# Attention with mixed heads and a gated feed-forward: keys loaded in rows of 768 bytes and transposed in seven pieces per pair, the last value rows loaded once and copied

## The chip, the cores and the metric

The kernel runs on one core of a Trainium2 chip. The metric is device time in microseconds (us) of one execution. Five engines of the core matter: TensorE (PE; its weight loads are shown apart as PEld), VectorE (DVE), ScalarE (ACT), GpSimd (POOL) and SyncE (SP), which here issues nearly all DMAs from one queue, in program order. A DMA that has to wait for a semaphore holds up every DMA behind it in that queue.

## The reference

```
scores = scale * q @ k^T                          # 4 batches, 12 heads, 448 positions, head size 64
scores = einsum('bhij,hg->bgij', scores, w_pre)   # heads are mixed before the softmax
attn   = softmax(scores)
attn   = einsum('bhij,hg->bgij', attn, w_post)    # and after it
x      = attn @ v                                 # as 1792 tokens x 768
out    = (silu(x @ w_gate) * (x @ w_val)) @ w_out # 768 -> 1536 -> 768
```

All inputs and the output are float32.

## The kernel before

Attention comes first (to about 411 us), batch by batch; the feed-forward part fills the rest. In attention the scores q k^T of all heads (`qk`, L275) are copied to SBUF (`stg`) and stored to DRAM (`s_all`, L294), so that they can be read back with heads and positions together on the partitions. `gather` (L305) reads the scores of 20 positions, a unit `u`, into a tile `rs`; a batch has 23 units. `pre` (L324) mixes the heads of the unit on TensorE, `top` and `expo` (L335, L341) make the softmax, `post` (L368) mixes the heads again and turns the result, and `av` (L410) multiplies by the values.

The keys of two heads, a pair, are loaded by `load_k` (L205; tile `kn`): 384 positions of the 448, three to a partition, and the last 64 of all heads in a load of their own (L192, and L202, tile `kl`). `kprep` (L228) turns a pair into the layout that `qk` wants, with transposes on TensorE into the PSUM tile `ktr`: three of 128x128 and one for the last 64 positions. `kcopy` takes the result to SBUF. There are 6 pairs in a batch and 24 in all.

The load of a pair before writes each partition in the order position, head, 64 numbers; a run of DRAM that stays together on both sides has 64 numbers, 256 bytes, so a pair has 128 x 6 = 768 such packets. The values (`load_v`, L170 and L176; tile `vn`) come in four loads of 384 positions in packets of 768 bytes, and two loads of the last 64 positions, one to partitions 0 to 63 and one to 64 to 127, in packets of 256 bytes (64 x 12 = 768 packets each), because `av` needs these rows on both halves.

The order of the program is a list of times written by hand: each step stands under a key, `at(key, fn)`, and the steps are sorted by it. A unit has two key units. Batch `b` starts at key `n0 = 45 b`; the keys of batch `b + 1` are loaded and turned during units 10 to 15 of batch `b`, and the values of batch `b` are loaded at keys `n0 + 16.2` to `n0 + 24.2`, so both loads meet in the same stretch of the SP queue with the gathers and the score stores. For batch 0 the keys of all pairs, the queries and the values are loaded in a prologue (negative keys) that ends with the first gathers.

Of the kernel before, what the change touches and what calls it, by code (L numbers as in the profile page):

```python
# [11 lines left out]
F32 = mybir.dt.float32  # L12
# [12 lines left out]
def talking_heads_moe_kernel(ctx, tc, q, k, v, w_pre, w_post, w_gate, w_val, w_out, out):  # L25
    nc = tc.nc
# [3 lines left out]
    P = 128  # L30
# [118 lines left out]
                wpost[half].rearrange("p g s -> p s g"), wq, n, op=ALU.mult  # L149
            )  # L150

    qn, kn, vn, kk, qt, stg, rs, pts, sts, et, rw, ats, trs, qtrs, qks = ({} for _ in range(15))


    def keys(c):
        return min(P, S - c * P)
# [7 lines left out]
    def load_v(b, c):  # L164
        full = S - PART
        if b not in vn:
            vn[b] = vp.tile([P, H, NC, D], F32, tag="vn", name=f"vn_{b}")
        if c < NC:
            hs = slice(c * (H // NC), (c + 1) * (H // NC))
            nc.sync.dma_start(  # L170
                out=vn[b][:, hs, :NC - 1].rearrange("p h c d -> p h (c d)"),
                in_=v[b, hs, :full].rearrange("h (p c) d -> p h (c d)", c=NC - 1),
            )
        else:
            r = c - NC
            nc.sync.dma_start(  # L176
                out=vn[b][r * HB:(r + 1) * HB, :, NC - 1], in_=v[b, :, full:].rearrange("h p d -> p h d")
            )

    def load_q(b, c, eng=nc.sync):  # L180
        m = scored(c)
# [3 lines left out]
    def load_k(b, p, part=None, eng=nc.sync):  # L185
        full = S - PART
        n = (NC - 1) * 2 * D
        if b == 0:
            if "all" not in kn:
                kn["all"] = stp.tile([P, NPAIR * NC * 2 * D], F32, tag="stg", name="kn_0")  # L190
            if part == 1:
                eng.dma_start(  # L192
                    out=kn["all"][:PART, NPAIR * n:].rearrange("p (h d) -> p h d", d=D),
                    in_=k[b, :, full:].rearrange("h p d -> p h d"),
                )
                return
            t = kn["all"][:, p * n:(p + 1) * n]
            last = kn["all"][:PART, NPAIR * n + p * 2 * D:NPAIR * n + (p + 1) * 2 * D]
        else:
            if p == 0:  # L200
                kn["last"] = nat.tile([PART, H, D], F32, tag="kl", name=f"kl_{b}")
                nc.sync.dma_start(out=kn["last"], in_=k[b, :, full:].rearrange("h p d -> p h d"))  # L202
            t = nat.tile([P, n], F32, tag="kn", name=f"kn_{b}_{p}", bufs=3)
            last = kn["last"][:, 2 * p:2 * p + 2].rearrange("p h d -> p (h d)")
        eng.dma_start(  # L205
            out=t.rearrange("p (c j d) -> p (c j) d", j=2, d=D),
            in_=k[b, 2 * p:2 * p + 2, :full].rearrange("j (p c) d -> p c j d", c=NC - 1),
        )
        kn[b, p] = [t[:, c * 2 * D:(c + 1) * 2 * D] for c in range(NC - 1)] + [last]

    def first_act():
        t = smp.tile([P, 1], F32, tag="st", name="first_act", bufs=4)
# [7 lines left out]
    def kprep(b, p):  # L220
        kt = kn.pop((b, p))
        if b == 0:
            tr = ps.tile([P, S], F32, tag="pre" if p in (2, 3) else "post", name=f"ktr_{b}_{p}")
        else:
            tr = ps.tile([P, S], F32, tag="tr", bufs=2, name=f"ktr_{b}_{p}")
        for c in range(NC):
            m = keys(c)
            nc.tensor.transpose(tr[:, c * P:c * P + m], kt[c], ident[:m, :m])  # L228
        trs[b, p] = tr

    def kcopy(b, p):
# [156 lines left out]
    def av(b, c0, m, p):  # L388
        n = -(-cols(c0, m) // TS)
        w = SEG // (3 - m)  # L390
        pt = [ps.tile([P, S], F32, tag="tr", name=f"av_{b}_{c0}_{p}_{r}")[:, :SEG] for r in range(2)]
        first = (b * NC + c0) % NSEG
        wrapped = first + m > NSEG
        ring = attnT.rearrange("p (s u) z i -> p s u z i", s=NSEG)
        u0 = first * SU
        for c in range(NC):
            for x in range(3 - m):
                for r in range(2):
                    k = (n + 1 - r) // 2
                    part = slice(r * HB, (r + 1) * HB) if c == NC - 1 else slice(P)  # L400
                    for j in range(2):
                        h = 2 * (p + x) + j
                        js = slice(j * D, (j + 1) * D)
                        if wrapped:
                            o = pt[r][js].rearrange("p (s u i) -> p s u i", s=2, i=TS)
                            a = ring[part, 0:NSEG:NSEG - 1, :, place(r, c) + h]
                        else:
                            o = pt[r][js, x * SEG // 2:x * SEG // 2 + k * TS].rearrange("p (u i) -> p u i", i=TS)
                            a = attnT[part, u0:u0 + k, place(r, c) + h]
                        nc.tensor.matmul(o, vn[b][part, h, c], a, start=(c == 0 and x == 0), stop=(c == NC - 1 and x == 2 - m))  # L410
        avs[b, c0, p] = pt, c0, m, wrapped

    def spread(av, *to):
# [96 lines left out]
    for b in range(B):  # L510
# [2 lines left out]
        def slot(u):  # L513
            return (n0 if u >= 0 else n0 - NTB) + 2 * (u if u >= 0 else u + NUB)

        for i, c in enumerate((NC, NC + 1, *range(NC))):
            at(n0 + 16.2 + 1.6 * i if b else (-34.3, -34.29, -30.35, -30.34, -29.35, -29.34)[i], later(load_v, b, c))
        if b == 0:
            at(-61.0, later(load_q, b, 0, nc.scalar))
            at(-60.9, first_act)  # L520
# [603 lines left out]
```

## Time and profile before

| | |
|---|---|
| time, median of 3 runs | 906.1 us (905.49 to 907.57) |
| the profiled execution's own time | 903.57 us |
| its span, first to last instruction | 901.9 us |
| mean granted TensorE clock | 0.979 of 2.4 GHz |
| TensorE busy | 858.8 us, 95% of the span |
| DMA, mean over the span | 242 GB/s, 187537 packets, 58360 of them under 512 bytes |
| wait of TensorE for gathers / for keys | 13.6 us / 4.0 us |

The profile counts an engine as busy from the start to the modelled end of each instruction, so a TensorE that is busy all the time can still be at half its clock: the granted clock stands in a column of its own. The DMA share is the mean over the 16 DMA engines and can pass 1 where packets of two queues overlap.

### The profile page before, as it was taken

Reading aid. Unit: us, or ns where it says so; the run is one execution under the profiler, and the core shown is the slowest. Engines: PE = TensorE matmul, PEld = TensorE weight load, DVE = VectorE, ACT = ScalarE, POOL = GpSimd, SP = SyncE. Lnnn points to the kernel's source line nnn. Section 1 sums busy time; section 2 is a strip of 40 time slices with the busy share of each in tenths; the row PEclk is TensorE's granted clock in tenths of the full one; section 3 lists DMA queues with packets and bytes.
Section 4 is the critical chain, followed back from the end, with each engine's and each line's share of the span. In section 5 each row is a group of like instructions: output and inputs, shape, how many; then the busy total and the mean of one; then the engine's idle time right before and its main releaser. Section 6 shows DMA issues by size and latency. Waiting matters only on the chain.

```text
span 901.9 us, 26545 instructions
## 1 busy us (share of the span) xinstructions
PE 858.8 (95%) x10886; PEld 706.9 (78%) x10886; DVE 647.6 (72%) x1204; ACT 457.8 (51%) x1042; POOL 177.0 (20%) x257
## 2 busy tenths in 40 slices
PE   8579999899989998989999999999999998999998
PEld 5355676566656665768999999999999998999998
DVE  3466576567656756575999999678899978766853
ACT  3375677567656767654333333354554464353321
POOL 2111111111211111113544543111001121002020
PEclk9699999899979999999999999999999999999999
DMA  9899988998898779544778776446655578988696
GB/s 214 289 304 283 272 295 245 318 301 280 281 320 256 242 253 291 186 133 152 254 231 265 242 259 225 145 157 212 220 178 178 187 275 285 347 268 195 171 306 156
DMA packets 187537, 218.03 MB, mean 242 GB/s; under 512 B 58360, under 2 KB 155160, under 8 KB 187416
## 3 DMA queue, kind: packets, MB, share of 16 engines
q1 hardware_dynamic: 181448, 207.97, 72.0%
q0 software_dynamic: 2080, 5.51, 3.5%
q10 hardware_dynamic: 3888, 2.86, 1.2%
q8 instruction: 86, 1.41, 0.6%
q14 instruction: 35, 0.29, 0.1%
HBM read 136.77 MB, written 79.54 MB: 240 GB/s over the span
## 4 chain that ended last, share of the span: by engine, by line
PE 81%; DMA 6%; DVE 6%; ACT 3%; issue 2%; SPq 1%; POOL 0%; ACTq 0%; POOLq 0%; DVEq 0%
PE pre L324 8%; PE av L410 8%; PE post L368 7%; PE p L758 6%; PE p L755 6%; PE p L756 6%; PE q L899 5%; PE q L897 5%; PE q L898 5%; PE qk L275 5%; DMA rs<-s_all 4%; PE upv L811 3%; PE upv L810 3%; PE upv L814 3%; PE upg L814 3%; PE upg L810 3%
## 5 line engine op out<-in xcount | busy, mean ns | idle before, releaser
L341 ACT ACTIVATE e<-pre,st 128x448 f32<-128x448 f32 x180 | 112.6, 630 | 91.8 <-DVE st L335 91.6
L660 POOL TENSOR_SCALAR mag<-mag 128x768 f32<-128x768 f32 x33 | 101.1, 3065 | 259.8 <-ACT mag L658 237.3
L335 DVE TENSOR_REDUCE st<-pre 128x1 f32<-128x448 f32 x180 | 104.5, 619 | 62.6 <-PE pre L324 58.4
L324 PE MATMUL pre<-rs,w_pre_blocks 64*64 64x448 f32 (+1 forms) x720 | 110.1, 579 | 18.0 <-DMA rs<-s_all 13.6
L368 PEld LDWEIGHTS post<-rw,e 60*64 60x64 f32 x5040 | 99.4, 138 | 33.4 <-issue 25.6
L352 POOL TENSOR_SCALAR rw<-w_post_gs,st 128x60 f32<-128x60 f32 x180 | 55.1, 320 | 325.3 <-DVE st L349 234.7
L368 PE MATMUL post<-rw,e 60*64 60x60 f32 x5040 | 106.7, 224 | 7.0 <-issue 3.9
L383 ACT ACTIVATE attnT<-post 128x420 f32<-128x420 f32 (+1 forms) x192 | 91.1, 541 | 23.8 <-PE post L368 23.1
L897 PE MATMUL q<-ohi,ah 128*128 128x384 f32 x276 | 93.6, 339 | 1.6 <-ACT ah L890 1.6
L899 PE MATMUL q<-ohi,al 128*128 128x384 f32 x276 | 93.8, 340 | 1.0 <-DVE al L882 1.0
L275 PE MATMUL qk<-kk,qt 64*64 64x448 f32 x672 | 93.4, 544 | 0.3 <-DVE w_post_gs L148 0.3
L898 PE MATMUL q<-olo,ah 128*128 128x384 f32 x276 | 93.5, 339 | 0.0
L410 PE MATMUL av<-attnT,vn 128*64 128x120 f32 (+9 forms) x1728 | 88.8, 262 | 3.0 <-DVE st L348 1.4
L410 PEld LDWEIGHTS av<-attnT,vn 128*64 128x64 f32 (+1 forms) x1728 | 70.4, 136 | 15.3 <-issue 5.6
L284 DVE COPY stg<-qk 128x448 f32<-128x448 f32 x120 | 71.1, 618 | 9.0 <-PE qk L275 4.2
L890 ACT ACTIVATE ah<-ar 128x768 fp32r<-128x768 f32 x46 | 38.6, 844 | 55.5 <-PE q L898 31.5
L275 PEld LDWEIGHTS qk<-kk,qt 64*64 64x64 f32 x672 | 32.2, 135 | 34.9 <-issue 24.1
L882 DVE TENSOR_TENSOR al<-ar,ah 128x768 fp32r<-128x768 f32 x46 | 43.9, 953 | 16.1 <-ACT ah L890 16.1
L324 PEld LDWEIGHTS pre<-rs,w_pre_blocks 64*64 64x64 f32 (+1 forms) x720 | 29.0, 138 | 33.2 <-issue 16.4
L899 PEld LDWEIGHTS q<-ohi,al 128*128 128x128 f32 x276 | 52.4, 190 | 2.0 <-DVE al L882 1.9
L897 PEld LDWEIGHTS q<-ohi,ah 128*128 128x128 f32 x276 | 52.3, 189 | 1.9 <-ACT ah L890 1.9
L810 PE MATMUL upv<-x,whi 128*128 128x448 f32 x144 | 52.8, 367 | 0.0
(142 smaller groups left out, 1688.5 us busy)
## 6 DMA issues: line engine op xcount, KB each, us to landing
rs<-s_all SPq DMA_DIRECT2D x88, 448.0 KB, 5.6
s_all<-stg SPq DMA_DIRECT2D x60, 448.0 KB, 4.8
w_d<-w SPq DMA_DIRECT2D x36, 384.0 KB, 4.3
raw<-in_moe_w_gate_dram SPq DMA_DIRECT2D x12, 768.0 KB, 5.5
raw<-in_moe_w_val_dram SPq DMA_DIRECT2D x12, 768.0 KB, 6.2
raw<-in_moe_w_out_dram SPq DMA_DIRECT2D x12, 768.0 KB, 6.4
w<-w_d SPq DMA_DIRECT2D x24, 384.0 KB, 5.5
s_all<-stg SPq DMA_DIRECT2D x39, 224.0 KB, 5.0
```

The lines of the kernel that those rows point to most:

```text
L275: nc.tensor.matmul(pt[x][i * HB:(i + 1) * HB], qt[b, c][hs, p, r:r + HB], kk[b, p][hs], start=True, stop=True)
L324: nc.tensor.matmul(pt[r][x * HB:(x + 1) * HB], wpre[i], xs[i, x], start=True, stop=True)
L335: nc.vector.tensor_reduce(sts[b, u][:, 0, r:r + 1], pts[b, t], axis=AX.X, op=ALU.max, negate=True)
L341: nc.scalar.activation(e, pts.pop((b, t)), AF.Exp, bias=st[:, 0, r:r + 1], scale=1.0, accum_out=st[:, 1, r:r + 1])
L368: nc.tensor.matmul(ats[b, u][y][o * HB:(o + 1) * HB, to, :m], et[b, t][i, c * P + x * HB:c * P + (x + 1) * HB], rw[b, t][i, :, :m], start= ...
L383: nc.scalar.activation(attnT[:part, i, n0:n1, y * HS:y * HS + m], pt[:part, n0:n1, :m], AF.Copy)
L410: nc.tensor.matmul(o, vn[b][part, h, c], a, start=(c == 0 and x == 0), stop=(c == NC - 1 and x == 2 - m))
L660: eng.tensor_scalar(mag, mag, f32_of(0x38000000), f32_of(0x47EFFFFF), op0=ALU.max, op1=ALU.min)
L810: nc.tensor.matmul(pt, hi[:, c], xh[:, c, ts], start=(c == 0), stop=False)
L897: nc.tensor.matmul(pt, ahi, bhi, start=f == 0, stop=False)
L898: nc.tensor.matmul(pt, ahi, blo, start=False, stop=False)
L899: nc.tensor.matmul(pt, alo, bhi, start=False, stop=f == NFH - 1)
```

## The change

Three edits. `load_k` writes each partition in the order head, position, so that the three positions of a partition, 768 bytes, are one packet: 256 packets for a pair in place of 768. The two heads' rows of one position no longer stand side by side, so `kprep` makes each of the three 128-position blocks with two transposes: one of 128 columns, whose upper half is head 1's row and whose lower half is a neighbouring row that isn't wanted there, and one of 64 columns that writes head 0's row over the lower half. Together with the last 64 positions that is seven transposes for a pair in place of four. The last positions of the values get a tile of their own, `vl`; one load fills its lower half, and `copy_v` copies this half to the upper one, from SBUF to SBUF, at key 1.55 in batch 0 and `n0 + 26.0` in the others.

```diff
@@ load_v
-            vn[b] = vp.tile([P, H, NC, D], F32, tag="vn", name=f"vn_{b}")
+            vn[b] = vp.tile([P, H, NC - 1, D], F32, tag="vn", name=f"vn_{b}")
+            vl[b] = vp.tile([P, H, D], F32, tag="vl", name=f"vl_{b}")
...
-            r = c - NC
-            nc.sync.dma_start(
-                out=vn[b][r * HB:(r + 1) * HB, :, NC - 1], in_=v[b, :, full:].rearrange("h p d -> p h d")
-            )
+            nc.sync.dma_start(out=vl[b][:HB], in_=v[b, :, full:].rearrange("h p d -> p h d"))
+
+    def copy_v(b):
+        nc.sync.dma_start(out=vl[b][HB:], in_=vl[b][:HB])
@@ load_k
         eng.dma_start(
-            out=t.rearrange("p (c j d) -> p (c j) d", j=2, d=D),
-            in_=k[b, 2 * p:2 * p + 2, :full].rearrange("j (p c) d -> p c j d", c=NC - 1),
+            out=t.rearrange("p (j z) -> p j z", j=2),
+            in_=k[b, 2 * p:2 * p + 2, :full].rearrange("j (p c) d -> p j (c d)", c=NC - 1),
         )
@@ kprep
-        for c in range(NC):
-            m = keys(c)
-            nc.tensor.transpose(tr[:, c * P:c * P + m], kt[c], ident[:m, :m])
+        t, last = kt
+        for c in range(NC - 1):
+            to = slice(c * P, (c + 1) * P)
+            nc.tensor.transpose(tr[:, to], t[:, (NC - 2 + c) * D:(NC + c) * D], ident)
+            nc.tensor.transpose(tr[:D, to], t[:, c * D:(c + 1) * D], ident)
+        nc.tensor.transpose(tr[:, (NC - 1) * P:], last, ident[:PART, :PART])
@@ the keys of the steps
-        for i, c in enumerate((NC, NC + 1, *range(NC))):
-            at(n0 + 16.2 + 1.6 * i if b else (-34.3, -34.29, -30.35, -30.34, -29.35, -29.34)[i], later(load_v, b, c))
+        for i, c in enumerate((NC, *range(NC))):
+            at(n0 + 16.2 + 1.6 * (i and i + 1) if b else (-34.3, -30.35, -30.34, -29.35, -29.34)[i], later(load_v, b, c))
+        at(n0 + 26.0 if b else 1.55, later(copy_v, b))
```

On TensorE, in the prologue, the first pair of keys stands like this before, from the queries' transposes to the second pair (`ktr` is the PSUM tile that is written, `kn` the keys):

```order
L245 MATMUL qtr_0_0_189<-ident,qn_0_118 128x64 x3
L228 MATMUL ktr_0_194<-ident,kn_120 128x128 x3
L228 MATMUL ktr_0_194<-ident,kn_120 128x64
L228 MATMUL ktr_1_201<-ident,kn_120 128x128 x3
L228 MATMUL ktr_1_201<-ident,kn_120 128x64
```

and with the change like this:

```order
L249 MATMUL qtr_0_0_189<-ident,qn_0_118 128x64 x3
L230 MATMUL ktr_0_194<-ident,kn_120 128x128
L231 MATMUL ktr_0_194<-ident,kn_120 64x128
L230 MATMUL ktr_0_194<-ident,kn_120 128x128
L231 MATMUL ktr_0_194<-ident,kn_120 64x128
L230 MATMUL ktr_0_194<-ident,kn_120 128x128
L231 MATMUL ktr_0_194<-ident,kn_120 64x128
L232 MATMUL ktr_0_194<-ident,kn_120 128x64
```

Every pair has three more transposes, whose output is 64 partitions by 128, and full and half ones alternate.

On the SP queue, in the prologue, the loads of values stand between the score stores; before:

```order
L294 DMA s_all<-stg_0_0_226 64x896
L183 DMA qn_2_231<-in_q_dram 128x12x64
L176 DMA vn_233<-in_v_dram 64x12x64 x2
L294 DMA s_all<-stg_0_1_263 64x896
L170 DMA vn_233<-in_v_dram 128x3x192 x2
L294 DMA s_all<-stg_0_2_276 64x896
L170 DMA vn_233<-in_v_dram 128x3x192 x2
L305 DMA rs_0_289<-s_all 128x2x448
```

and with the change:

```order
L298 DMA s_all<-stg_0_0_235 64x896
L184 DMA qn_2_240<-in_q_dram 128x12x64
L176 DMA vl_243<-in_v_dram 64x12x64
L298 DMA s_all<-stg_0_1_281 64x896
L171 DMA vn_242<-in_v_dram 128x3x192 x2
L298 DMA s_all<-stg_0_2_294 64x896
L171 DMA vn_242<-in_v_dram 128x3x192 x2
L309 DMA rs_0_307<-s_all 128x2x448
```

One load of the last value rows is gone ahead of the second score store; the rest keeps its order.

On the same queue in batch 1, where the keys of batch 2 and the values of batch 1 are loaded, from the gather of unit 11 to that of unit 13; before:

```order
L305 DMA rs_11_2636<-s_all 128x2x448
L176 DMA vn_2638<-in_v_dram 64x12x64
L205 DMA kn_1_2661<-in_k_dram 128x6x64
L294 DMA s_all<-stg_3_2_2652 128x896
L176 DMA vn_2638<-in_v_dram 64x12x64
L305 DMA rs_12_2709<-s_all 128x2x448
L205 DMA kn_2_2729<-in_k_dram 128x6x64
L170 DMA vn_2638<-in_v_dram 128x3x192
L294 DMA s_all<-stg_3_3_2723 128x896
L305 DMA rs_13_2775<-s_all 128x2x448
```

and with the change:

```order
L309 DMA rs_11_2673<-s_all 128x2x448
L176 DMA vl_2676<-in_v_dram 64x12x64
L206 DMA kn_1_2699<-in_k_dram 128x2x192
L298 DMA s_all<-stg_3_2_2690 128x896
L309 DMA rs_12_2746<-s_all 128x2x448
L206 DMA kn_2_2766<-in_k_dram 128x2x192
L171 DMA vn_2675<-in_v_dram 128x3x192
L298 DMA s_all<-stg_3_3_2760 128x896
L309 DMA rs_13_2812<-s_all 128x2x448
```

The second load of last value rows is gone from its place right ahead of the gather of unit 12; the copy stands further down, between the gathers of units 16 and 17.

## Rows read from the trace of the kernel before

**Rows 1.** The page: DMA share in 40 slices, in tenths.

```profile
DMA  9899988998898779544778776446655578988696
```

**Rows 2.** Stretches: us; busy PE, PEld, DVE, ACT, POOL; granted clock, DMA share, GB/s.

```profile
22.00:44.00 22.00, 12.64 (x176) 6.31 (x175) 9.67 (x22) 7.97 (x22) 1.80 (x6) 0.69 0.89 296
60.00:75.00 15.00, 10.48 (x236) 6.63 (x232) 8.57 (x22) 7.67 (x21) 2.12 (x8) 1.00 1.13 336
145.00:175.00 30.00, 27.48 (x589) 17.05 (x589) 18.13 (x47) 19.87 (x59) 4.78 (x16) 0.89 1.03 309
240.00:270.00 30.00, 26.45 (x553) 16.66 (x549) 18.87 (x52) 18.19 (x52) 5.29 (x17) 0.84 1.04 313
340.00:360.00 20.00, 16.81 (x439) 10.62 (x432) 13.39 (x35) 15.17 (x40) 3.58 (x12) 0.99 0.95 303
411.00:740.00 329.00, 328.76 (x1695) 301.86 (x1692) 282.50 (x387) 142.62 (x215) 92.10 (x30) 1.00 0.66 212
```

**Rows 3.** Waits of TensorE in attention: total us, times, longest.

```profile
PE pre L324 <- DMA rs<-s_all: 13.6, 6, 7.9
PE ktr L228 <- DMA kn<-in_k_dram: 4.0, 3, 3.1
```

**Rows 4.** Timeline of TensorE in batches 1 and 2; idle time before in brackets.

```profile
163.65 0.98 PE L324 MATMUL pre<-rs,w_pre_blocks 64*64 64x448 f32 x8 [0.41 <-DMA rs<-s_all]
165.87 0.52 PE L228 MATMUL ktr<-ident,kn 128*128 128x128 f32 x3 [1.24 <-DVE st L335]
168.63 1.77 PE L324 MATMUL pre<-rs,w_pre_blocks 64*64 64x448 f32 x8 [0.88 <-DMA rs<-s_all]
259.83 1.01 PE L324 MATMUL pre<-rs,w_pre_blocks 64*64 64x448 f32 x8 [2.93 <-DMA rs<-s_all]
264.12 1.77 PE L324 MATMUL pre<-rs,w_pre_blocks 64*64 64x448 f32 x8
```

**Rows 5.** Timeline of SP in the two crowded stretches of batches 1 and 2.

```profile
156.36 1.01 SPq L176 DMA_DIRECT2D vn<-in_v_dram  x1
157.42 1.49 SPq L305 DMA_DIRECT2D rs<-s_all  x1
161.08 0.44 SPq L305 DMA_DIRECT2D rs<-s_all  x1
252.47 0.60 SPq L176 DMA_DIRECT2D vn<-in_v_dram  x1
```

**Rows 6.** Transposes: durations at L228 (ns, min/median/max); timeline in the prologue.

```profile
L228 PE MATMUL ktr<-ident,kn x78: 272/273/473, 6.6 to 276.6; 128*128 128x128 f32 x72, 64*128 64x64 f32 x6
...
11.22 0.51 PEld L228 LDWEIGHTS ktr<-ident,kn 64*128 64x128 f32 x4 [0.17 <-issue]
11.90 0.51 PEld L228 LDWEIGHTS ktr<-ident,kn 64*128 64x128 f32 x4 [0.17 <-issue]
14.48 0.87 PE L245 MATMUL qtr<-ident,qn 128*128 128x128 f32 x6
```

**Rows 7.** DMA queue 1 in 10:12, 16:18 and 20:22: packets, MB, share.

```profile
q1 hardware_dynamic: 1381, 0.35, 107.3%
...
q1 hardware_dynamic: 1503, 0.38, 96.5%
...
q1 hardware_dynamic: 693, 0.55, 86.1%
```

**Rows 8.** Timeline of DVE and SP in the prologue.

```profile
12.85 3.56 SPq L176 DMA_DIRECT2D vn<-in_v_dram  x2
...
13.92 1.38 DVE L284 COPY stg<-qk 128x448 f32<-128x448 f32 x2 [0.40 <-PE qk L275]
...
16.52 1.03 SPq L294 DMA_DIRECT2D s_all<-stg  x1
...
19.09 0.56 SPq L294 DMA_DIRECT2D s_all<-stg  x1
...
25.09 1.64 SPq L305 DMA_DIRECT2D rs<-s_all  x3
```

More of the change, by code (lines that the diff above doesn't have):

```diff
@@ L150, in mixing_blocks @@
             )
-    qn, kn, vn, kk, qt, stg, rs, pts, sts, et, rw, ats, trs, qtrs, qks = ({} for _ in range(15))
+    qn, kn, vn, vl, kk, qt, stg, rs, pts, sts, et, rw, ats, trs, qtrs, qks = ({} for _ in range(16))
     def keys(c):
@@ L170, in load_v @@
             nc.sync.dma_start(
-                out=vn[b][:, hs, :NC - 1].rearrange("p h c d -> p h (c d)"),
+                out=vn[b][:, hs].rearrange("p h c d -> p h (c d)"),
                 in_=v[b, hs, :full].rearrange("h (p c) d -> p h (c d)", c=NC - 1),
@@ L205, in load_k @@
         eng.dma_start(
-            out=t.rearrange("p (c j d) -> p (c j) d", j=2, d=D),
-            in_=k[b, 2 * p:2 * p + 2, :full].rearrange("j (p c) d -> p c j d", c=NC - 1),
+            out=t.rearrange("p (j z) -> p j z", j=2),
+            in_=k[b, 2 * p:2 * p + 2, :full].rearrange("j (p c) d -> p j (c d)", c=NC - 1),
         )
-        kn[b, p] = [t[:, c * 2 * D:(c + 1) * 2 * D] for c in range(NC - 1)] + [last]
+        kn[b, p] = t, last
     def first_act():
@@ L409, in av @@
                             a = attnT[part, u0:u0 + k, place(r, c) + h]
-                        nc.tensor.matmul(o, vn[b][part, h, c], a, start=(c == 0 and x == 0), stop=(c == NC - 1 and x == 2 - m))
+                        nc.tensor.matmul(o, vn[b][part, h, c] if c < NC - 1 else vl[b][part, h], a, start=(c == 0 and x == 0), stop=(c == NC - 1 and x == 2 - m))
         avs[b, c0, p] = pt, c0, m, wrapped
```

## The prediction, made before the changed kernel ran

> **What bounds the kernel now.** I read the page's line of DMA shares first, then a table by stretch, the waits of TensorE, and the timelines of TensorE and SP at the places that the first three point to. The feed-forward part can be set aside: from 411 to 740 us TensorE is busy 328.76 of 329 us at full clock [rows 2], and the change touches nothing there. In attention the DMA engines are busy nearly throughout [rows 1], and two things cost TensorE time. One is plain waiting: 13.6 us for gathers and 4.0 us for keys [rows 3]. The other is the granted clock: it is 0.69 in 22 to 44 us, 0.89 in 145 to 175 and 0.84 in 240 to 270 [rows 2]. The chip grants 2.4 or 1.2 GHz, so a mean of 0.89 over 30 us is 30 x 0.11 / 0.5 = 6.6 us at half clock, and 0.84 is 9.6 us. Rows 4 show what goes before: in batch 1 TensorE idles 0.41, 1.24 and 0.88 us, and the same eight matmuls of `pre` that took 0.98 us take 1.77 us behind it; in batch 2 it idles 2.93 us, and `pre` takes 1.77 us from 264.12 on [rows 4]. So a stall there is paid twice, as idle time and as half clock behind it.
>
> Both places are the stretches where the keys of the next batch and the values of this one are loaded: DMA share 1.03 and 1.04 [rows 2], and SP takes 1.01 us to issue one load of last value rows right ahead of the gather of unit 12, which itself takes 1.49 us [rows 5]. Batch 0 has its crowded stretch at 60 to 75 us: share 1.13, TensorE busy 10.48 of 15 us [rows 2], 3.1 us of it waiting for the first keys [rows 3]. In batch 3, 340 to 360 us, values are loaded but no keys: busy 16.81 of 20 us [rows 2].
>
> **Transposes.** 24 pairs get 3 more each, 72. Six transposes of 128x128 in a row take 0.87 us [rows 6]; five steps and a last one that runs 0.27 us (the median there) make (0.87 - 0.27) / 5 = 0.12 us from start to start; I take 0.11, since the first step of a row waits for its weights. A pair takes 11.90 - 11.22 = 0.68 us before [rows 6]: four at 0.11 are 0.44, and the rest, 0.24, is two changes of shape (full to 64-row and back), 0.12 us each. Whether a 64-column piece changes the shape of the array too, no row shows. If it doesn't, a pair costs 3 x 0.11 = 0.33 us more; if every alternation costs one, there are five changes more, 0.60, and a pair costs 0.93 us more. I take 0.33, nearest to the transposes that keep all 128 rows: 72 x 0.11 = 7.9 us over the kernel, 2.0 us for the keys of each batch. The upper end is 22 us.
>
> The Trainium skill, page "TensorEngine Tiling (Array Packing)", Key Properties and Restrictions, says that a change of tiling mode drains the engine, and that column tiling cannot be combined with the transpose mode for float32. The drain agrees with the 0.12 us of [rows 6]; by the second rule the 64-column piece runs on the whole array, without a change of shape, at the lower end, 7.9 us.
>
> **Key loads.** A packet of 256 bytes costs: 1381 packets in 107.3% of 16 engines for 2 us is 24.9 ns each at the end of the loads of keys and queries, and 1503 in 96.5% is 20.5 ns a little later; 693 packets of 790 bytes in the mean, in 86.1%, is 39.8 ns [rows 7]. So a pair takes 768 x 20.5 / 16 = 0.98 us of all DMA engines before and 256 x 39.8 / 16 = 0.64 after: 0.35 us less (0.56 by the dearer row), 2.1 us in a batch.
>
> The Trainium skill, page "DMA: Bandwidth & Descriptors", section "Why small descriptors are slow (HBM only)", puts a packet at one cycle for 32 bytes and about 3 more: 3 x 11 = 33 cycles before against 27 after. By that rule a load shrinks by 18%, 0.18 us as an estimate, half of what the rows give, and the time would end nearer to no change. The 24.9 ns against 39.8 [rows 7] speak for the larger figure.
>
> **Last value rows.** The second load is 768 packets of 256 bytes as well: 0.98 us of DMA less in each batch, and on SP one issue less (0.60 to 1.01 us in [rows 5]; two took 3.56 us in the prologue [rows 8]). The copy adds 192 KB in 64 packets: 0.55 MB took 0.861 x 2 us [rows 7], so 0.6 us, and one issue, 0.44 us like a gather's [rows 5]. In batches 1 to 3 it stands behind the crowded stretch, between the gathers of units 16 and 17, and `av` needs it 3.3 key units later, some 7 us (411 us are 180 key units); in batch 0 it stands at key 1.55 and `av` starts at 29.3. The gather of unit 17 goes out 0.4 us later for it, and its `pre` is due some six key units behind. I take no wait of TensorE for either. If it landed late, `av` would wait perhaps 1 to 2 us a batch.
>
> **Place by place**, with the sum.
>
> Prologue. The first gather goes out at 25.09 us, when the third score store, issued at 19.09, has landed [rows 8]. SP was the late one: its second store went out at 16.52, though the data were ready at about 14.6 (the first of the two copies that start at 13.92) [rows 8]. Without one load, SP is free near 14.6; but the six pairs' transposes, 18 x 0.11 = 2.0 us, delay the data, less the two waits for keys that the shorter loads end (4.0 - 3.1 = 0.9 us [rows 3]): 1.1 us, so data at 15.7, store 0.8 us earlier. The copy gives back 0.4 us on SP. Net -0.5 us (from +1 to -1.5, and more if the half-clock stretch shortens as well).
>
> Batch 0, 60 to 85 us: +2.0 us of transposes, the 3.1 us wait for the first keys shorter by about 1.0 (0.35 for the load itself, the rest its issue behind fewer packets). Net +1.0.
>
> Batch 1: ahead of the gather of unit 13 (issued at 161.08, its `pre` at 168.63 [rows 4, 5]) lie three key loads and the dropped value load: 3 x 0.35 + 0.98 = 2.0 us of DMA, and SP a little earlier. I take 2.2 of the idle time of 0.41 + 1.24 + 0.88 = 2.5 us [rows 4]. Transposes +2.0. Net -0.2, before the clock.
>
> Batch 2: two key loads and the value load lie ahead of the gather that TensorE waits 2.93 us for [rows 4]: 2 x 0.35 + 0.98 = 1.7. Transposes +2.0. Net +0.3, before the clock.
>
> Batch 3: no keys; the value load alone, -0.9.
>
> Clock. In batch 1 the 6.6 us at half clock are full of work: at full clock 3.3 us less. In batch 2 those from 264.12 to 270 us are, 5.9 us: 2.9 us less. I take one of the two dips as gone: -3.1.
>
> Sum: -0.5 + 1.0 - 0.2 + 0.3 - 0.9 - 3.1 = -3.4 us. The profiled execution took 903.57 us, 2.5 below the median of the runs, and I let the difference carry over: 903.57 - 3.4 = 900.2, and in the median 906.1 - 3.4 = 902.7 us.
>
> **Rivals.**
>
> Both dips go, and the half-clock stretch of the prologue, 22 x 0.31 / 0.5 = 13.6 us [rows 2], shortens by half a dip: -3.4 - 3.1 - 1.7 = -8.2, 897.9 us. For it speaks that TensorE's stalls in batch 1 are already short; against it, that the DMA stays the bound of these stretches (share 1.03 and 1.04 [rows 2]), so TensorE at full clock would run into the next gather.
>
> The stalls shrink, but the clock dips as before: -3.4 + 3.1 = -0.3, 905.8 us. If a part of the 20.5 ns is other queues' traffic and not the packet's size, and a load saves only half of 0.35 us, it ends here too: 6 x 0.17 = 1.0 us of relief less in each of three batches, a part of it on the path, up to 908.
>
> Slower: the transposes lie on the path in full. This is one mechanism, TensorE as the bound: if the gathers' landing is set by when their scores were stored and not by how full the DMA queues are, the relief of the queues buys nothing in batches 0 to 2 and the 7.9 us stay, less 1.4 for prologue and batch 3 (0.5 + 0.9): 912.6 us. It decides as soon as less than 2.0 us of idle time and half clock go from a crowded stretch. For it: between stretches TensorE has hardly any idle time, so any work that is not covered by a stall counts. Against: the transposes stand in just the stretches in which TensorE idles.
>
> Slower still: every alternation of full and half transposes costs a change of shape: 24 x 0.60 = 14.4 us on top of the forecast, 917.1 us. Nothing in the rows excludes it.
>
> The change not doing what it says is no case: packets and transposes are fixed by the program.
>
> **How the numbers follow.** Chances: forecast 0.38 (its own range 900 to 904.3), both dips gone 0.17 (894 to 900), dips stay 0.22 (904 to 908), transposes on the path 0.15 (908 to 914), changes of shape 0.08 (914 and more). The range of 8 in 10 leaves out the lower third of the second case and the upper part of the last two: 896 to 911 us. Within 0.2%, 904.3 to 907.9 us, is about what a measurement of this kernel cannot tell from no change. Faster: 0.38 + 0.17 + 0.05 of the third = 0.60. Same: the rest of the third, 0.17. Slower: 0.15 + 0.08 = 0.23.
>
> **What the profile after would show.** Starts 0.11 us apart through the six alternating transposes of a pair, a pair near 1.0 us (0.2 us apart would be the changes of shape). Key packets of 768 bytes and some 15,000 fewer packets (24 x 512 and 4 x 704). The wait for `rs` below 13.6 us, the idle times at 163 to 168 and 257 us nearly gone, the clock of 145 to 175 or of 240 to 270 us near 1. The first gather on SP at 24 to 25 us. The prediction is wrong if the gathers' landing times stay and TensorE's span in a batch grows by 2 us, if `av` waits for `vl`, or if a dip appears in a place that had none.

## The result, and the profile after

The changed kernel takes 910.93 us (median of 12 runs, 906.09 to 916.76); the kernel before took 905.15 us beside it (12 runs). The ratio is 1.0086, 95% interval [1.0058, 1.0114]: slower by some 7.8 us (5.8 us between the medians), where 3.4 us faster was forecast. The time lies at the upper edge of the stated range (896 to 911), on the side that had 0.23 of the chances. The profiled execution took 911.61 us, its span is 909.9 us, its mean granted clock 0.983.

The page of the kernel after: busy time of TensorE and the DMA line, in the form of [rows 1].

```profile
PE 866.7 (95%) x10958; PEld 713.7 (78%) x10958; DVE 651.0 (72%) x1204; ACT 458.1 (50%) x1042; POOL 175.9 (19%) x257
...
DMA packets 172433, 218.03 MB, mean 240 GB/s; under 512 B 36856, under 2 KB 139800, under 8 KB 172312
```

The 72 transposes and the 15,104 packets less are there. TensorE is busy 7.9 us longer than before (858.8), and its span is 8.0 us longer: the idle time is the same, 43 us. That both figures stand near the 7.9 us that the transposes are long is no proof that these are the cause; the places below show another. What TensorE is idle for has changed. Waits of TensorE in attention, after:

```profile
PE pre L328 <- DMA rs<-s_all: 9.9, 4, 5.4
PE av L414 <- DMA vl<-vl: 5.0, 3, 2.6
...
PE qtr L249 <- DVE x_t L489: 2.4, 1, 2.4
...
PE ktr L230 <- DMA kn<-in_k_dram: 1.6, 2, 1.2
```

The waits for gathers and keys fell by 3.7 and 2.4 us [rows 3]. Of the 3.7 us, 2.5 are no gain: they lie ahead of the first gather (7.9 us of waiting before, 5.4 after), where the first `pre` starts at 30.35 us and no earlier than the 30.23 of before. In their place stands a wait that the kernel before didn't have: `av` waits 5.0 us for the copy of the last value rows, once in each of batches 1 to 3 (2.63, 2.10 and 0.32 us).

The stretches right behind the crowded ones, before, with columns as in [rows 2]:

```profile
175.00:190.00 15.00, 14.86 (x323) 9.81 (x319) 9.19 (x26) 9.14 (x26) 2.49 (x7) 0.99 0.90 271
270.00:290.00 20.00, 19.80 (x438) 13.01 (x433) 11.98 (x40) 12.61 (x43) 2.39 (x8) 0.98 0.88 255
```

These and the stretches of [rows 2], after:

```profile
60.00:75.00 15.00, 12.70 (x299) 7.94 (x292) 10.16 (x26) 9.85 (x26) 2.02 (x7) 1.00 1.08 345
145.00:175.00 30.00, 29.13 (x669) 19.41 (x662) 20.62 (x50) 21.84 (x66) 4.78 (x16) 1.00 0.99 317
175.00:190.00 15.00, 12.37 (x252) 8.14 (x246) 6.79 (x20) 5.78 (x17) 1.88 (x5) 0.89 0.80 237
240.00:270.00 30.00, 24.43 (x531) 15.96 (x532) 18.30 (x53) 18.05 (x51) 4.81 (x15) 0.94 0.90 274
270.00:290.00 20.00, 17.62 (x294) 11.10 (x296) 8.42 (x25) 8.72 (x27) 1.79 (x6) 0.75 0.82 255
```

Two of the crowded stretches got better: in 60 to 75 and 145 to 175 us TensorE is busy 12.70 and 29.13 us, where it was 10.48 and 27.48, and the clock of 145 to 175 is 1.00, where it was 0.89 [rows 2]. (Batch 3 can't be read in this way: after is 8 to 9 us late there, so 340 to 360 us holds earlier units than before.) A loss comes right behind: in 175 to 190 us TensorE is busy 12.37 us at a clock of 0.89, where it was 14.86 at 0.99, and in 270 to 290 us it is busy 17.62 at 0.75, where it was 19.80 at 0.98.

Not all of that lies at one place. A mean of 0.75 over 20 us is 10 us at half clock. Of these, 6.5 stand behind a wait for a gather (2.23 us, ended at 268.38): the clock is 0.51 in 269.6 to 276.5 us. The other 3.4 us, 283.3 to 286.7, come later. The timeline of TensorE shows what stands ahead of the half clock in batch 1:

```profile
176.76 0.42 PE L414 MATMUL av<-attnT,vl 64*64 64x120 f32 x4
179.81 0.32 PE L414 MATMUL av<-attnT,vl 64*64 64x120 f32 x2 [2.63 <-DMA vl<-vl]
...
180.70 1.76 PE L279 MATMUL qk<-kk,qt 64*64 64x448 f32 x8
```

The four matmuls of `av` that read the loaded half of `vl` run; those that read the copied half wait 2.63 us, and the eight matmuls of `qk` behind them take 1.76 us, where they took 0.93 before at full clock. Batch 2 has the same at 282.10, after 2.10 us. Behind each of the two waits the clock is 0.50 for 3.4 us (180.9 to 184.3 and 283.3 to 286.7), which costs 1.7 us. So the late copy is paid twice, as [rows 4] showed it of late gathers: 5.0 us of waiting and 3.4 us of clock, 8.4 us.

Counting by work and not by time gives the same place. From the first `pre` of unit 14 to that of unit 17, with the copy's wait between them, batch 1 took 173.00 to 189.29 us before and 171.69 to 191.75 after, 3.8 us more; batch 2 took 268.71 to 284.79 before and 272.81 to 293.82 after, 4.9 us more. In e1 below, where the copy is early, the same two sections take 0.1 and 0.3 us less than before.

The queue of SP says why the copy is late:

```profile
168.23 3.36 SPq L171 DMA_DIRECT2D vn<-in_v_dram  x1
171.68 2.00 SPq L206 DMA_DIRECT2D kn<-in_k_dram  x1
...
175.13 0.53 SPq L179 DMA_DIRECT2D vl<-vl  x1
```

The last value load and the last key load hold SP for 5.4 us. The copy goes out at 175.13, and `av` goes on at 179.81, 4.7 us later (5.5 in batch 2); it wants the data at 179.81 - 2.63 = 177.18. The copy needs 4.7 us and has 2.05. The trace of before held the same warning: its last value load took SP 3.12 us from 170.64 and its last key load 1.88 us from 173.87.

### The profile page after: what moved, and what is told of

Its sections match the earlier page's. It is cut to its first block, busy times and chain, and to the rows that moved or that the text cites. A ratio compares the mean times of both kernels' runs of the same rounds, so it can differ in the third digit from the quotient of the medians.

```text
span 909.9 us, 26684 instructions
## 1 busy us (share of the span) xinstructions
PE 866.7 (95%) x10958; PEld 713.7 (78%) x10958; DVE 651.0 (72%) x1204; ACT 458.1 (50%) x1042; POOL 175.9 (19%) x257
## 4 chain that ended last, share of the span: by engine, by line
PE 81%; DMA 8%; DVE 5%; ACT 3%; issue 2%; SPq 1%; POOL 0%; ACTq 0%; DVEq 0%; POOLq 0%
PE pre L328 7%; PE post L372 7%; PE av L414 7%; PE p L763 6%; PE p L761 6%; PE p L760 6%; PE qk L279 5%; PE q L904 5%; PE q L903 5%; PE q L902 5%; PE upv L816 3%; PE upv L815 3%; PE upv L819 3%; PE upg L819 3%; PE upg L815 3%; PE upg L816 3%
## 5 line engine op out<-in xcount | busy, mean ns | idle before, releaser
L328 PE MATMUL pre<-rs,w_pre_blocks 64*64 64x448 f32 (+1 forms) x720 | 106.0, 567 | 16.1 <-DMA rs<-s_all 9.9
L372 PE MATMUL post<-rw,e 60*64 60x60 f32 x5040 | 104.8, 223 | 5.4 <-issue 3.8
L414 PE MATMUL av<-attnT,vn 128*64 128x120 f32 (+5 forms) x1296 | 70.2, 257 | 2.1 <-DVE st L352 0.8
L414 PEld LDWEIGHTS av<-attnT,vn 128*64 128x64 f32 x1296 | 59.1, 136 | 7.1 <-DVE qt L256 2.4
L816 PE MATMUL upv<-x,wlo 128*128 128x448 f32 x144 | 53.0, 368 | 0.0
L815 PE MATMUL upg<-x,whi 128*128 128x448 f32 x144 | 52.9, 368 | 0.0
```

Source lines behind the costliest of these rows:

```text
L328: nc.tensor.matmul(pt[r][x * HB:(x + 1) * HB], wpre[i], xs[i, x], start=True, stop=True)
L372: nc.tensor.matmul(ats[b, u][y][o * HB:(o + 1) * HB, to, :m], et[b, t][i, c * P + x * HB:c * P + (x + 1) * HB], rw[b, t][i, :, :m], start= ...
L414: nc.tensor.matmul(o, vn[b][part, h, c] if c < NC - 1 else vl[b][part, h], a, start=(c == 0 and x == 0), stop=(c == NC - 1 and x == 2 - m))
L815: nc.tensor.matmul(pt, hi[:, c], xh[:, c, ts], start=(c == 0), stop=False)
L816: nc.tensor.matmul(pt, lo[:, c], xh[:, c, ts], start=False, stop=False)
```

## The experiments

How they are read: beside the ratio, the table gives two sums over the waits of TensorE in the profiled execution, from 0 to 411 us: waits that a DMA ended, and waits that the profile puts down to nothing it shows ("issue"). The last two columns are means over all runs of the kernel, less those of the kernel before on the same chip: the time lost to the clock is span x (1 - mean granted clock), "rest" is the span without it. Their standard errors are near 1 us, for the kernels with 6 runs up to 1.5. For after these columns stay empty: the runs of before beside it have no clock on record. The sums of waits are of one execution, which can lie over 6 us off its kernel's median (e4: 912.17 against 905.8; e8: 899.24 against 905.51), so they say where a kernel waits and don't add up to its time.

| kernel | median, us (runs) | ratio to before | DMA / issue, us | clock / rest, us |
|---|---|---|---|---|
| before | | | 17.6 / 5.4 | |
| after | 910.93 (12) | 1.0086 [1.0058, 1.0114] | 16.5 / 4.3 | |
| e1_copy_early | 901.08 (12) | 0.9992 [0.9965, 1.0019] | 11.5 / 11.4 | -3.4 / +3.0 |
| e2_keys_only | 904.51 (12) | 1.0024 [0.9998, 1.005] | 12.8 / 11.5 | -0.7 / +3.0 |
| e3_values_only | 914.62 (6) | 1.0115 [1.007, 1.0161] | 25.2 / 5.2 | +4.5 / +6.4 |
| e4_transposes_only | 905.8 (12) | 1.005 [1.0023, 1.0076] | 16.6 / 10.8 | -0.3 / +5.4 |
| e5_packets_only | 901.99 (12) | 0.9997 [0.9968, 1.0026] | 17.9 / 5.6 | -0.4 / -0.3 |
| e6_values_copy_early | 904.35 (12) | 1.0026 [1.0003, 1.005] | 18.1 / 8.0 | +0.7 / +0.6 |
| e7_copy_from_gpsimd | 903.17 (12) | 1.0018 [0.9998, 1.0038] | 11.9 / 7.5 | -3.2 / +4.0 |
| e8_copy_ahead_of_last_loads | 905.51 (12) | 1.0022 [0.9991, 1.0053] | 10.8 / 8.7 | -2.2 / +3.9 |
| e9_copy_later | 915.76 (6) | 1.0164 [1.0124, 1.0204] | 23.3 / 5.3 | +2.6 / +12.2 |
| e10_copy_early_everywhere | 904.58 (12) | 1.004 [1.0014, 1.0066] | 9.8 / 12.6 | -1.5 / +5.3 |
| e11_pad_32 | 902.34 (10) | 1.0022 [0.9991, 1.0052] | 5.9 / 9.1 | -2.4 / +4.2 |
| e12_pad_64 | 908.33 (10) | 1.007 [1.0033, 1.0107] | 4.3 / 13.3 | -0.7 / +7.2 |

### The place of the copy: e1, e7, e8, e9, e10

**The copy 4.5 key units earlier (e1).**

```diff
-        at(n0 + 26.0 if b else 1.55, later(copy_v, b))
+        at(n0 + 21.5 if b else 1.55, later(copy_v, b))
```

> The changed kernel with one number changed: the copy of the last value rows at key n0 + 21.5 in place of n0 + 26.0 in batches 1 to 3, so that it stands ahead of the gather of unit 14 and not behind that of unit 16. Theory A (TensorE lost its time to the copy: av waited 2.6 and 2.1 us for it in batches 1 and 2, and about half of two dips of 3.4 us at half clock behind it): av no longer waits for vl, and the time is 903 to 908 us, 4 to 7 below the changed kernel. Theory B (the 72 added transposes lie on the path in full): the wait goes, but the time stays at 909 to 912 us.

The wait for the copy is gone and with it the whole loss: 0.9992, even below the 903 to 908 us of theory A. Its SP queue, and the same two stretches as above:

```profile
162.07 0.70 SPq L179 DMA_DIRECT2D vl<-vl  x1
...
168.77 3.24 SPq L171 DMA_DIRECT2D vn<-in_v_dram  x1
172.10 1.84 SPq L206 DMA_DIRECT2D kn<-in_k_dram  x1
```

```profile
175.00:190.00 15.00, 14.71 (x342) 10.20 (x338) 8.56 (x27) 8.06 (x24) 2.49 (x7) 1.00 0.90 275
...
270.00:290.00 20.00, 19.47 (x468) 13.97 (x460) 12.13 (x42) 12.63 (x45) 2.39 (x8) 1.00 0.88 276
```

4.5 key units earlier in the program is 13.1 us earlier on SP, since the two long loads now stand behind the copy. Behind the crowded stretches TensorE is busy 14.71 and 19.47 us at full clock.

**The same key, another queue (e7).**

```diff
-        nc.sync.dma_start(out=vl[b][HB:], in_=vl[b][:HB])
+        (nc.gpsimd if b else nc.sync).dma_start(out=vl[b][HB:], in_=vl[b][:HB])
```

> The changed kernel with the copy at its place, n0 + 26.0, but issued by GpSimd in batches 1 to 3, whose queue holds nothing else there than the scaling of w_post for unit 12. If the copy was late because SP's queue was late (its issue at 175.13 us, av needing it from 177 us): it goes out 4 to 7 us earlier against its batch, av waits less than 1 us, and the time is near that of the early copy, 900 to 905 us. If the copy itself is slow: av waits as long as before, 908 us or more.

With the copy under its old key, but issued by GpSimd, it goes out at 168.66, 6.5 us before SP got to it, and no wait is put down to it any more:

```profile
168.66 0.58 POOL L179 DMA_DIRECT2D vl<-vl  x1
```

So it is what stands ahead of the copy in SP's queue that makes it late, and not its key.

**Ahead of the last value load and the last key load (e8).** The edit is the key `n0 + 24.15`.

> The changed kernel with the copy at n0 + 24.15, two places up the SP queue: ahead of the last value load and the last key load, which held SP for 3.36 and 2.00 us in batch 1, and behind everything else as before. If these two held it up: the copy goes out some 6 us earlier, av does not wait, and the time is near that of the early copy, 900 to 905 us. If the lateness lies further up the queue: av still waits 1 us or more in batches 1 and 2.

```profile
165.67 3.65 SPq L179 DMA_DIRECT2D vl<-vl  x1
169.36 0.59 SPq L171 DMA_DIRECT2D vn<-in_v_dram  x1
170.04 1.67 SPq L206 DMA_DIRECT2D kn<-in_k_dram  x1
```

SP is now held for 3.65 us at the copy, and the value load behind it, which took 3.36 us, takes 0.59. The delay belongs to the place in the queue, not to the load that stands there. The copy lands late from there too, 8.7 and 9.6 us after its issue began in batches 1 and 2; `av` still waits once, 1.3 us, and 905.51 us is just above what was expected without a wait.

What the place has in common in all 14 kernels is the DMA ahead of it: the load of queries (`qn`, 128 x 12 rows of 256 bytes). What stands right behind it there, in batches 1 and 2, takes SP 2.6 to 4.7 us; behind the other loads of queries the next DMA mostly takes 0.3 to 2 us, so such a load alone doesn't do it. No run moved it, and why the place is slow isn't shown.

**Behind one more gather (e9).** The edit is the key `n0 + 29.2`.

> The changed kernel with the copy one place further down the SP queue, key n0 + 29.2, behind the gather of unit 17. If the wait of av for the copy sets the loss: the copy goes out 0.7 to 1.2 us later in each of batches 1 to 3, av waits about 1 us longer in each, and the time is 1 to 4 us above the changed kernel, 912 to 915 us where it takes 911. If the wait only takes the place of another one: no difference to the changed kernel.

The copy goes out at 176.90, 1.8 us later, and the wait grows from 5.0 to 12.2 us:

```profile
PE av L414 <- DMA vl<-vl: 12.2, 3, 5.3
```

Part of the 1.8 us is SP, which ran 1.1 us later up to there. The wait grew by 7.2 us, where about 3 were expected, and the time follows, 1.0164, 915.76 us where 912 to 915 were. With e1 this makes three doses of one cause: no wait 0.9992, 5.0 us 1.0086, 12.2 us 1.0164.

**Early in batch 0 too (e10).** The edit drops the case for batch 0: `at(n0 + 21.5, later(copy_v, b))`.

> The changed kernel with the copy at n0 + 21.5 in all batches, so that in batch 0 it leaves the crowded start (key 1.55, ahead of the gather of unit 4, which TensorE waited 1.96 us for in the changed kernel's profile). If the copy in the prologue costs what that wait shows: 1 to 2 us below the version with the early copy in batches 1 to 3 alone, so 0.1 to 0.3% faster than before. If not: within 1 us of that version.

At 1.0040 it isn't better than e1, so moving the copy out of the prologue gives nothing back. Its ratio is even 0.5% above e1's, where a time within 1 us of e1's or below it was expected; why stays open.

### The parts by themselves: e2 to e6

**Keys alone (e2), values alone (e3).** The kernel before with one half of the diff each, as it stands in the section on the change.

> The kernel before with the keys' edit alone: 768-byte packets and seven transposes for a pair; the last value rows are loaded twice as before. Theory A: within 3 us of before, since the relief of the DMA queues pays for the transposes. Theory B: 6 to 8 us slower than before, 911 to 913 us.

> The kernel before with the values' edit alone: last value rows loaded once and copied at n0 + 26.0; keys as before. Theory A: av waits for vl in batches 1 and 2, some 2 us each, and the time is 2 to 6 us above before. Theory B: one DMA load less in each batch and no transposes, so 0 to 3 us below before.

The loss sits in the values: 1.0115 against 1.0024. It is larger than the 2 to 6 us that theory A gave it, some 10 us. In e3 SP issues the copy at 172.09, 3.0 us before after's, but TensorE is at this `av` 3.8 us earlier too, at 173.34, and it waits 12.4 us in all, in each of batches 1 to 3; in batch 1:

```profile
177.43 0.47 PE L411 MATMUL av<-attnT,vl 64*64 64x120 f32 x2 [4.09 <-DMA vl<-vl]
```

**Values alone with the early copy (e6).** e3 with the key `n0 + 21.5`.

> The kernel before with the values' edit alone and the copy at n0 + 21.5. If the late copy is the whole loss of that edit: no wait of av for vl, and 1 to 4 us below before, 10 to 14 below the same edit with the copy at n0 + 26.0. If one value load less is worth nothing: within 1 us of before.

1.0026: of the 1.15% some 0.9 are back without the late copy, and `av` has no wait for `vl`. But neither expectation was met: one load less doesn't make the kernel faster, the time is some 2 us above before, and the waits for DMAs (18.1 us) are those of before.

**Transposes alone (e4).** The kernel before, with three more half transposes for a pair, which write over what is there with the same numbers.

```diff
             nc.tensor.transpose(tr[:, c * P:c * P + m], kt[c], ident[:m, :m])
+            if c < NC - 1:
+                nc.tensor.transpose(tr[:D, c * P:(c + 1) * P], kt[c][:, :D], ident)
```

> The kernel before with three more transposes of 64 columns for each pair, which write again what stands there already; loads as before. It prices the 72 transposes without any relief. Theory A: 2 to 6 us slower than before, since part of them lies in the idle time of the crowded stretches. Theory B: 7 to 9 us slower.

0.5% or 4.5 us [2.1, 6.9] for 72 transposes, 5.4 us by the last column: two thirds of the 7.9 us that they are long.

**Packets alone (e5).** The kernel before with after's two lines in `load_k` and no edit to the transposes, so that the keys come out in a wrong order.

> The kernel before with the keys in 768-byte packets but still four transposes of the same shapes for a pair; these transposes take their columns from the new layout as if it were the old one, so the keys stand in a wrong order in the scores and the output isn't the reference's. It prices the relief of the DMA queues without its cost on TensorE. If the relief pays for most of the transposes (they cost 4.5 us alone): 1 to 4 us below before. If the relief buys nothing: within 1 us of before, and the keys' edit would have to cost the full 4.5 us.

0.9997: loads in packets of 768 bytes, without any transposes to pay for them, are worth nothing that this measurement tells from no change. The waits for DMAs stay at 17.9 us in its profile, though the clock is 1.00 in both 145 to 175 and 240 to 270 us.

### Where the relief went: e11 and e12

With the extra transposes and no late copy (e1) the waits that a DMA ends fall from 17.6 to 11.5 us, but those put down to "issue" rise from 5.4 to 11.4. The rows of before, and of e1:

```profile
PE post L368 <- issue: 3.9, 5, 1.2
PE pre L324 <- issue: 1.3, 2, 1.0
```

```profile
PE post L372 <- issue: 8.3, 7, 2.4
PE pre L328 <- DMA rs<-s_all: 7.8, 3, 5.8
PE ktr L230 <- DMA kn<-in_k_dram: 3.7, 4, 2.3
...
PE av L414 <- issue: 2.5, 4, 1.4
```

The page lists a DMA queue of its own for instructions:

```profile
q8 instruction: 86, 1.41, 0.6%
```

That is 16 KB a packet; with two instructions for each of some 10,950 matmuls a packet holds near 256, or 128 matmuls. If these gaps are packets that come late, a shift of the program by some instructions has to move them. e11 and e12 are e1 with 32 and 64 small matmuls ahead of the first `pre` of batch 0, where TensorE waits for its first gather:

```diff
+        if b == 0 and u == 0:
+            for _ in range(32):    # 64 in the other
+                nc.tensor.matmul(pt[0][:HB, :8], ident[:, :HB], ident[:, :8], start=True, stop=True)
```

> The change with the copy at key n0 + 21.5, and 32 small extra matmuls (8 columns each, into a PSUM tile that pre overwrites right behind them) ahead of the first pre of batch 0, in the 5.7 us that TensorE waits there for its first gather; they change no result. They shift every later instruction of TensorE by 64. Question: with extra transposes and no wait for the copy, the waits of TensorE that the profile puts down to nothing it shows (issue) rise from 5.4 us before to 11.4 us, and eat what the shorter waits for gathers and keys (17.6 to 11.5) gave. The page lists 86 packets of 16 KB of instructions (1.41 MB; TensorE has 10958 matmuls and as many weight loads), so a packet holds some 256 instructions. Theory A: these gaps are instruction packets that arrive late while the DMA engines are full; then the gaps of the copy-early kernel at 351.4 (ahead of post, 55 of 56 matmuls done), 363.9 and 370.2 us (ahead of post with 38 left) come about 32 matmuls earlier in the program, and their sum changes, to anything from 5 to 13 us. Theory B: something in the order of the program holds TensorE there; then the gaps stay ahead of the same matmuls, and the sum stays near 11. Time within 4 us of 901 either way.

> As the kernel with 32 extra matmuls, but 64 of them, so every later instruction of TensorE is shifted by 128, half of a packet of 256 instructions. Theory A (late instruction packets): the gaps come about 64 matmuls earlier in the program than in the copy-early kernel, so none stands ahead of the same matmul, and the sum changes. Theory B (the order of the program): the same matmuls, the sum near 11 us. Time within 4 us of 901; if A holds and a shift moves the gaps to where TensorE has slack, up to 5 us less.

Each of them stands in the trace as two matmuls (64 rows for the 32), so the shifts are 128 and 256 instructions, half a packet and a whole one, and not a quarter and a half as written above. By theory A the gaps of e11 must then stand half a packet away from e1's, and those of e12 ahead of the same matmuls as e1's. Timelines of TensorE in batch 3, e1, then e12, then e11:

```profile
351.40 0.26 PE L372 MATMUL post<-rw,e 60*64 60x60 f32 x1 [2.36 <-issue]
...
357.15 0.33 PE L372 MATMUL post<-rw,e 60*64 60x60 f32 x3 [0.53 <-issue]
...
370.22 0.80 PE L372 MATMUL post<-rw,e 60*64 60x60 f32 x38 [1.51 <-issue]
```

```profile
359.00 0.21 PE L375 MATMUL post<-rw,e 60*64 60x60 f32 x1 [1.48 <-issue]
...
364.77 0.32 PE L375 MATMUL post<-rw,e 60*64 60x60 f32 x3 [0.54 <-issue]
...
377.55 0.80 PE L375 MATMUL post<-rw,e 60*64 60x60 f32 x38 [1.50 <-issue]
```

```profile
353.73 0.27 PE L375 MATMUL post<-rw,e 60*64 60x60 f32 x2 [0.83 <-issue]
...
364.10 0.33 PE L375 MATMUL post<-rw,e 60*64 60x60 f32 x5 [1.68 <-issue]
364.36 1.45 PE L417 MATMUL av<-attnT,vn 128*64 128x120 f32 x24
365.74 0.44 PE L417 MATMUL av<-attnT,vl 64*64 64x120 f32 x8
366.00 0.93 PE L331 MATMUL pre<-rs,w_pre_blocks 64*64 64x448 f32 x8
366.75 0.99 PE L375 MATMUL post<-rw,e 60*64 60x60 f32 x56
367.67 1.45 PE L417 MATMUL av<-attnT,vn 128*64 128x120 f32 x24
369.05 0.42 PE L417 MATMUL av<-attnT,vl 64*64 64x120 f32 x2
370.48 0.33 PE L417 MATMUL av<-attnT,vl 64*64 64x120 f32 x3 [1.01 <-issue]
```

e12 has its gaps ahead of the last 1, 3 and 38 matmuls of a `post`, where e1 has them, some 7.5 us later. e11 has them half a packet away: from its gap at 364.10 to the place in `post` with 38 matmuls left there are 5 + 24 + 8 + 8 + 18 = 63 matmuls, and from there to its next gap 38 + 24 + 2 = 64. Between two gaps of e1 lie one packet's matmuls, by the table of stretches that begin and end at gaps (second column: busy time of TensorE and its matmuls):

```profile
351.40:357.15 5.75, 4.47 (x126) 2.90 (x126) 2.66 (x6) 4.05 (x11) 0.60 (x2) 1.00 0.84 297
357.15:363.90 6.75, 5.38 (x128) 4.26 (x128) 2.58 (x9) 3.94 (x12) 1.20 (x4) 1.00 1.01 345
363.90:370.22 6.32, 4.81 (x126) 3.85 (x127) 2.96 (x9) 3.71 (x11) 0.60 (x2) 1.00 0.81 297
```

The trace has the packets of this queue too. In e1 four of them are through at 350.02, 355.71, 362.41 and 368.78 us, and TensorE goes on at 351.40, 357.15, 363.90 and 370.22, each time 1.4 to 1.5 us later. In all 14 kernels every such gap of 0.5 us or more, 94 in number, ends 1.2 to 1.7 us behind a packet of this queue. So the gaps are TensorE at the end of a packet of instructions, with the next one not there yet; theory B falls. What makes a packet late, no run tests.

Over these three kernels the waits for DMAs go 11.5, 5.9, 4.3 us and these gaps 11.4, 9.1, 13.3. Most of the fall in the first row is the first gather's wait (5.75, 1.50 and 0 us), which the small matmuls fill. e12 missed its expected time, 908.33 for 901 +- 4: its 128 matmuls ran from 24.69 to 35.87 us, the later ones at half clock (0.50 in 30 to 40), where the first `pre` of e1 starts at 29.32.

## Why the prediction was wrong

The step that failed is this: "I take no wait of TensorE for either." It gave the copy "some 7 us" because `av` stands 3.3 key units behind it. Key units are the order of the program; SP ran late behind its two long loads, so 7 us were 2.05 us for a copy that takes 4.7, and the 0.6 us of DMA time in the prediction is not its time to landing. The prediction saw the danger ("If it landed late, `av` would wait perhaps 1 to 2 us a batch", and `av` waiting for `vl` as a sign of failure) but gave it no price in the sum, no clock behind it and no chance. It measured 5.0 us of waiting and 3.4 us of half clock behind it in one profile, 8.4 us, and 8.5 us in the ratios of after and e1 (0.0094 x 905), with some 3.5 us of error either way. That this is the cause is shown: with the copy early the loss is gone (e1), with another queue too (e7), values alone bring it (e3) and lose most of it again (e6), and a later copy nearly doubles it (e9).

**Transposes.** Right in their length. The first four starts in a row of six, after:

```profile
162.57 0.33 PE L230 MATMUL ktr<-ident,kn 128*128 128x128 f32 x1
162.73 0.27 PE L231 MATMUL ktr<-ident,kn 128*64 128x128 f32 x1
162.84 0.27 PE L230 MATMUL ktr<-ident,kn 128*128 128x128 f32 x1
162.95 0.27 PE L231 MATMUL ktr<-ident,kn 128*64 128x128 f32 x1
```

From the second on they are 0.11 us apart, the same step for 128 and for 64 columns, so no change of shape shows. That agrees with the rule of the Trainium skill that the prediction weighed (page "TensorEngine Tiling (Array Packing)", Restrictions). The 917.1 us of that rival are out. The time of after lies near the rival "transposes on the path", 912.6 us, but not by its mechanism: e1 has all the transposes and 0.9992. A part of that mechanism is at work, though, as the sum below shows.

**Packets.** Their number was right, their worth not: e5 shows none. Keys' packets and transposes together (e2) cost 3.0 us of rest, transposes alone 5.4, so here the packets gave back some 2.4 us, with errors as large as the difference.

**Prologue.** The first gather goes out at 24.68 us, 0.4 us earlier than in [rows 8], forecast 0.5. That the two are close is luck: the store that should have gone 0.8 us earlier went 0.16 us later, at 16.68: the one load ahead of it goes out 1.03 us later, at 13.88, and takes SP 2.69 us, where two took 3.56 [rows 8]. And the first `pre` starts 0.12 us later than before.

**Places.** In batches 0 and 1 the idle time went down about as forecast (the stretches above). In batch 3 the forecast 0.9 us didn't come: after is 7.7 us behind before at the first `pre` of its unit 10 and 8.0 at that of unit 18. In batch 2 of after TensorE was idle longer, with a wait of 2.37 us for `x_t` ahead of `qtr` and one of 2.23 us for a gather; in e1 the same `x_t` takes 0.5 us. One profile shows it and no experiment was aimed at it, so its cause stays open.

**Clock.** The forecast was -3.1 us for one of two dips. Without the late copy the full change loses less to the clock than before in every version: 3.4 (e1), 3.2 (e7), 2.2 (e8), 1.5 (e10), 2.4 (e11) and 0.7 us (e12). So the size is about right, at its upper end. In after the dip of batch 1 went behind the copy, and batch 2 has three: behind the wait for `x_t` (0.50 in 249.2 to 252.6 us), behind a gather and behind the copy. The sign of failure that the prediction named, a dip in a place that had none, came true in e1 as well: its clock in 60 to 75 us is 0.89, where it was 1.00 [rows 2]. The base was not typical: the profiled execution of before lost 901.9 x 0.021 = 18.9 us to the clock, the runs of before beside e1 and e5 12.9 and 13.8 in the mean. Why keys and values alone (e2, e6) bring none of it and both together do, the runs don't tell.

**The sum.** Free of the late copy the forecast would still have been too good: e1 is at 0.9992, within [-3.2, +1.7] us of before, where -3.4 was forecast. The terms by place, transposes included, were to give -0.3 us; the rest is +3.0 in e1, +4.0 in e7 and +3.9 in e8. So the second step that failed is the relief: it was to pay for the transposes in full, and paid, within the errors, for less than half of the 5.4 us that they cost alone (e4). One way in which it got lost is shown in e1: 6.1 us less of waiting for DMAs stand against 6.0 us more at the ends of instruction packets, since a TensorE that no gather stops runs on to the end of its packet and waits there. It isn't the whole of it: in e7 and e8 both sums together are 3.6 and 3.5 us below before, and the rest is still 4 us above. No version that was run beats the kernel before by more than the measurement tells.

## What to carry to other kernels

Measure the slack of a new DMA in microseconds of the queue that issues it, at the place where it will stand, and not in steps of the program: a copy that takes 4.7 us behind two loads that hold the queue for 5.4 is late, and the same copy well ahead of them, or from an idle queue, brings no wait. When a load is replaced by a load and a dependent copy, put the copy where its source is ready, not where its reader is near. And when a wait for data is taken away, look at the gaps that the profile explains by nothing: here the instructions themselves were the next thing to come late.

## What the runs showed of the hardware

- **One place of SP's queue costs 2.6 to 4.7 us whatever stands there.** In batch 1 the issue of the last value load took 3.12 us (before), 3.36 (after), 3.24 (e1), and with the copy in that place the copy took 3.65 and the load 0.59 (e8); in batch 2 of after the load took 4.43. In all 14 kernels the place is right behind one load of queries, in batches 1 and 2.
- **Instructions of TensorE come in packets of 16 KB, and their lateness shows as gaps without a releaser** 126 to 128 matmuls apart in batch 3, up to 2.36 us each in e1, in stretches where the DMA share is 0.8 to 1.0. Each ends 1.2 to 1.7 us after a packet of that queue is through. A shift of 256 instructions brought them back to the same matmuls, one of 128 moved them.
- **A float32 transpose of 64 columns beside one of 128** costs the same step, 0.11 us, and no change of shape shows (after).
- **A copy of 192 KB within SBUF** from SP took 4.1 to 4.4 us from issue to landing at 36 us (after, e1, e3, e6, e8, e9), and 6.8 to 9.6 us in the crowded stretches of batches 1 and 2 (e1, e6, e8, e10); from GpSimd it took 6.0 to 7.5 (e7). Behind the crowded stretch its reader went on 4.7 to 6.1 us after the issue (after, e3, e9).
